# Attention and squared-ReLU MLP on one core: a maximum traced ahead of a subtraction, and v loaded a head sooner

## The chip, the cores and the metric

The kernel runs on one core of a Trainium2 chip. The metric is the device time of one execution in microseconds (us), and lower is better. Before the change the median of three executions is 1206.76 us (1206.62 to 1213.95). The engines are called PE (TensorE, matmuls), PEld (its weight loads), DVE (VectorE), ACT (ScalarE), POOL (GpSimd) and SP (SyncE, which here only issues transfers).

## The reference

Sixty-four heads (8 batches of 8) of causal attention with a decay, 576 positions, 64 columns each; then an MLP over 4608 tokens.

```python
scores = scale * np.matmul(q, k.transpose(0, 1, 3, 2))
cum = np.cumsum(np.log(np.clip(f, 0.0001, 1.0)), axis=-1)
scores = np.where(causal, -1000000000.0, scores + cum[:, :, :, None] - cum[:, :, None, :])
scores = scores - np.max(scores, axis=-1, keepdims=True)
attn = np.exp(scores)
attn = attn / (np.sum(attn, axis=-1, keepdims=True) + 1e-09)
attn_out = np.matmul(attn, v)
h = np.maximum(x @ w_in, 0.0)          # x is attn_out, heads side by side, (4608, 512)
out = (h * h @ w_out)                  # w_in (512, 2048), w_out (2048, 512)
```

The weights are double precision in memory; everything else is single precision.

## The kernel before, in words

The 64 heads are worked off one after the other, each in six slots (`NU` = 6). In a slot a head's scores are made for one stretch of queries and keys (`score`, L423 to L433), ACT turns them into exponentials (L440), and two slots later they are multiplied with v (`av_part`, L487, or L466 to L468 from head 16 on). One head ahead of its scores, each row's maximum is found from a cheaper matmul: `max_units` makes six units a head, each of them a matmul on PE (L376) into a PSUM bank and a reduction on DVE out of that bank (L384, two instructions, the second of which writes the result column `tcol`). The next user of the bank has to wait for the reduction. From the point at which the MLP's chunk 1 begins until chunk 2 begins, scores and maxima take turns in only two banks, so that a unit's matmul waits for the reduction of the unit before it.

How q and k are prepared depends on the head. Heads 0 to 9 load them rounded through POOL's queue (`load_rounded`, L292) and whole through SP's (`load_whole`, L299), and their scores are one matmul of unrounded numbers. For heads 10 to 63, `load` (L277) brings one raw tile `qkraw`, of which there is only one buffer, and `prep` splits it in four parts: part 0 rounds q and k on DVE (L321, L322) and copies the rounded k by a transfer (L323), part 1 copies the rounded q by another (L327), part 2 subtracts the rounded k from the raw one and part 3 does the same with q. For heads 10 to 19 the two subtractions run on DVE (L329 and L333, 64 x 576 each). From head 20 on `prep_split` does them on POOL.

v is loaded per head into a tile `v` of three buffers (`load_v`: the transfer L306 on SP, and on POOL a memset of its last two columns, L308). The tile comes free when the matmuls with v of the head three before are done.

Beside attention runs the MLP, chunk by chunk (L591, L606 to L609, L621), and, until about 220 us, the conversion of its weights on ACT and DVE (L206 to L242), whose loads (L195, 512 KB each) go through SP.

The order of PE, ACT, DVE and POOL is the order in which the program is traced (`in_order`). It is laid out by slots: `at(n, half, ...)` puts a step into the first or second half of slot n, and steps that fall into one half are traced in the order in which `at` was called. So the order of the calls in the loop over heads matters, not only the numbers in them. SP's order is left to the scheduler of the tile framework. An SP row that has to wait holds up everything behind it. Before the change the calls for a split head put part 1 and part 2 of `prep` into slot 1, second half, where the first maximum (unit 0) also falls, and part 3 into slot 3, second half, with unit 4; slots here count from the start of the head before.

Of the kernel before, what the change touches and what calls it, by code (L numbers as in the profile page):

```python
# [34 lines left out]
def decay_attention_relu2_kernel(  # L35
# [38 lines left out]
    NWHOLE = 10  # L74
# [195 lines left out]
    NU = len(UNITS)  # L270
# [407 lines left out]
    SPLIT = 0, 1, 1, 3  # L678
    LOAD = 4
    VLOAD, VSPLIT = 2, 4  # L680
# [56 lines left out]
    def at(n, half, do, *args):  # L737
        events.setdefault((n, half), []).append(lambda: do(*args))
# [6 lines left out]
    for h in range(NH):  # L745
        split = h >= NWHOLE
        if split:
            at((h - 2) * NU + LOAD, 0, load, h)
            for part in range(4):
                at((h - 1) * NU + SPLIT[part], 1, prep, h, part)  # L750
        else:
            if h > 1:
                at((h - 3) * NU + 3, 0, load_rounded, h)
                at((h - 2) * NU + 5, 1, load_whole, h)
        at((h - 1) * NU + VLOAD, 1, load_v, h)
        at((h - 1) * NU + VSPLIT, 1, split_v, h)
        for i, x in enumerate(MAXIMA[split]):
            at((h - 1) * NU + int(x), int(2 * x) % 2, max_unit, h, i)
        if not split:
            at((h - 1) * NU + (4 if h else 3), 0, turn_maxima, h)  # L760
    for b in range(B):
# [25 lines left out]
    for n in range(-2 * NU, last_slot + 1):  # L787
        live = 0 <= n < len(slots)
        split_last()
        if live:  # L790
            h, u = slots[n]
# [65 lines left out]
```

## Time and profile before

| | us |
|---|---|
| median of three executions | 1206.76 |
| the profiled execution | 1208.21 |
| its span, first to last instruction | 1206.5 |
| PE busy | 1178.1 (98%) |
| DVE busy | 784.9 (65%) |
| ACT busy | 684.6 (57%) |
| POOL busy | 316.9 (26%) |
| mean granted TensorE clock | 0.997 |

Busy shares are of the whole span; in the stretch from 90 to 260 us, where the weights are converted beside attention and MLP, DVE is busy for about 83% of the time, and nearly without a gap for stretches of ten or more. A timeline row gives the start in us, the duration in us, the engine, the line and the tiles, written tile first; in brackets stands how long the engine was idle before it and what ended that. A row of a wait table gives who waited for whom, us in total, how often, and the longest. In a table of stretches each engine has its busy time and its count, and at the end stand the granted clock, the DMA share and the GB/s.

### The profile page before, as it was taken

How to read it: one execution, taken by the hardware profiler on the slowest of the kernel's cores; microseconds unless marked ns; L12 is line 12 of the kernel's file. 1: busy time of each engine (PE TensorE's matmuls, PEld its weight loads, DVE VectorE, ACT ScalarE, POOL GpSimd, SP SyncE). 2: the span in 40 equal slices, each digit the busy share in tenths (PEclk: the TensorE clock that was granted, in tenths of full speed). 3: DMA queues.
4: the chain of work that ended last, by engine and by line, in shares of the span. 5: the costliest groups of instructions: out<-in, count | busy, mean ns of one | idle time of the engine just before them, and what ended most of it. 6: DMA issues, size and time to landing. Idle time of an engine off the chain costs nothing. (4 is left out here: it accounts for less than half of the span.)

```text
span 1206.5 us, 23195 instructions
## 1 busy us (share of the span) xinstructions
PE 1178.1 (98%) x7786; PEld 1040.9 (86%) x7786; DVE 784.9 (65%) x2096; ACT 684.6 (57%) x1716; POOL 316.9 (26%) x511
## 2 busy tenths in 40 slices
PE   8999999999999999999999999999999999999998
PEld 4667877789998989899999899988999899999997
DVE  5889987766766676666656667666666766543332
ACT  3765555546666566656565566666566666533232
POOL 2110000213434343422222343334333434200000
PEclk9999999999999999999999999999999999999999
DMA  7785722221212121111110212112121112000000
GB/s 204 194 209 165 196 54 46 74 67 35 51 42 60 42 55 43 50 42 35 36 50 17 59 38 54 38 43 59 42 54 36 47 42 59 12 28 18 1 19 18
DMA packets 109798, 73.33 MB, mean 61 GB/s; under 512 B 90720, under 2 KB 90720, under 8 KB 109680
## 3 DMA queue, kind: packets, MB, share of 16 engines
q1 hardware_dynamic: 108880, 68.90, 22.4%
q0 software_dynamic: 800, 2.95, 1.1%
q8 instruction: 62, 1.02, 0.4%
q14 instruction: 56, 0.46, 0.1%
HBM read 58.71 MB, written 9.87 MB: 57 GB/s over the span
## 5 line engine op out<-in xcount | busy, mean ns | idle before, releaser
L621 PE MATMUL bank<-w,gh 128*128 128x512 f32 x1152 | 413.5, 399 | 0.0
L591 PE MATMUL bank<-xh,w 128*128 128x256 f32 x2304 | 331.6, 286 | 5.3 <-ACT r L606 5.1
L591 PEld LDWEIGHTS bank<-xh,w 128*128 128x128 f32 x2304 | 300.1, 189 | 16.8 <-ACT r L606 9.3
L456 DVE TENSOR_TENSOR pl<-p,ph 128x320 fp32r<-128x320 f32 (+4 forms) x288 | 175.4, 610 | 200.6 <-ACT ph L455 195.1
L621 PEld LDWEIGHTS bank<-w,gh 128*128 128x128 f32 x1152 | 217.5, 189 | 37.9
L621 PE MATMUL bank<-w,gl 128*128 128x512 f32 x576 | 227.1, 394 | 0.2 <-DVE gl L609 0.2
L455 ACT CAST ph<-p 128x320 fp32r<-128x320 f32 (+4 forms) x288 | 119.4, 415 | 162.0 <-POOL p L442 119.2
L607 DVE TENSOR_TENSOR g<-r 128x256 f32<-128x256 f32 x288 | 124.3, 432 | 102.0 <-ACT r L606 101.7
L442 POOL TENSOR_SCALAR_AFFINE_SELECT p<-p 128x128 f32<-128x128 f32 (+1 forms) x240 | 85.9, 358 | 396.1 <-ACT p L440 328.2
L606 ACT ACTIVATE r<-bank 128x256 f32<-128x256 f32 x288 | 109.7, 381 | 137.1 <-PE bank L591 124.5
L591 PE MATMUL bank<-xl,w 128*128 128x256 f32 x1152 | 184.8, 283 | 0.0
L440 ACT ACTIVATE p<-bank 128x320 f32<-128x320 f32 (+4 forms) x288 | 111.2, 386 | 117.9 <-PE bank L428 105.9
L384 DVE CUSTOM_DVE_ANT_0 bank<-bank,mz 128x256 f32<-128x256 f32 (+4 forms) x320 | 133.6, 431 | 50.6 <-PE bank L376 50.2
L609 DVE TENSOR_TENSOR gl<-g,gh 128x256 fp32r<-128x256 f32 x288 | 139.1, 483 | 34.4 <-PE bank L621 1.0
L591 PEld LDWEIGHTS bank<-xl,w 128*128 128x128 f32 x1152 | 158.5, 191 | 0.2 <-DVE xl L577 0.2
L608 ACT ACTIVATE gh<-r 128x256 fp32r<-128x256 f32 x288 | 120.4, 418 | 9.2
L376 PE MATMUL bank<-rk 66*128 66x320 f32 (+4 forms) x384 | 109.1, 314 | 13.4 <-DVE tcol L384 8.4
L621 PEld LDWEIGHTS bank<-w,gl 128*128 128x128 f32 x576 | 109.2, 190 | 15.0 <-DVE gl L609 1.7
L428 PE MATMUL bank<-rl 128*128 128x320 f32 x324 | 95.1, 294 | 0.0
L425 PE MATMUL bank<-rk 67*128 67x320 f32 x324 | 93.4, 288 | 0.0
L376 PEld LDWEIGHTS bank<-rk 66*128 66x128 f32 (+1 forms) x384 | 67.1, 181 | 30.4 <-DVE tcol L384 12.8
L466 PE MATMUL bank<-pl,vh 128*65 128x320 f32 (+4 forms) x336 | 91.3, 272 | 0.0
(97 smaller groups left out, 1478.8 us busy)
## 6 DMA issues: line engine op xcount, KB each, us to landing
qkraw<-in_qk SPq DMA_DIRECT2D x54, 288.0 KB
v<-in_v SPq DMA_DIRECT2D x64, 160.0 KB
out<-osb SPq DMA_DIRECT2D x36, 256.0 KB
den<-rdr SPq DMA_DIRECT2D x62, 144.0 KB
w<-in_w_in SPq DMA_DIRECT2D x16, 512.0 KB
w<-in_w_out SPq DMA_DIRECT2D x16, 512.0 KB
rk<-tcol SPq DMA_DIRECT2D x216, 0.5 KB
rl<-in_qk SPq DMA_DIRECT2D x10, 288.0 KB
```

Source lines behind the costliest of these rows:

```text
L376: nc.tensor.matmul(ps[:m, :n], st["r2"][:D + 2, q0:q0 + m], st["kl0"][:D + 2, k0:k0 + n], start=True, stop=True,)
L384: nc.vector.tensor_tensor_reduce(out=ps[:m, :n], in0=ps[:m, :n], in1=mz[:m, mo:mo + n], op0=ALU.add, op1=ALU.min, scale=-1.0, scalar=init, ...
L428: nc.tensor.matmul(ps[:kn, :n], st["l2"][:, k0:k0 + kn], st["r1"][:, q0:q1], start=False, stop=not added,)
L440: nc.scalar.activation(out=p[:kn, :n], in_=ps[:kn, :n], func=AF.Exp, scale=SCALE)
L455: nc.scalar.copy(out=ph[:kn, :n], in_=p[:kn, :n])
L456: nc.vector.tensor_tensor(out=pl[:kn, :n], in0=p[:kn, :n], in1=ph[:kn, :n].bitcast(F32), op=ALU.subtract,)
L591: nc.tensor.matmul(ph[:, :T], w[:, s, cc], x[:, cc, :], start=(cc == 0 and k == 0), stop=(cc == NCC - 1 and k == 2),)
L606: nc.scalar.activation(out=r, in_=ph[:, :T], func=AF.Relu)
L607: nc.vector.tensor_tensor(out=g, in0=r, in1=r, op=ALU.mult)
L608: nc.scalar.activation(out=gh, in_=r, func=AF.Square)
L609: nc.vector.tensor_tensor(out=gl, in0=g, in1=gh.bitcast(F32), op=ALU.subtract)
L621: nc.tensor.matmul(po, g[:, ts], w[:, s], start=(fc == 0 and k == 0), stop=(fc == NF - 1 and k == 2),)
```

## The change: two steps called elsewhere in the loop over heads

For split heads (10 and up) the four calls of `prep` move behind those of `max_unit`. Nothing else about them changes, so they stay in their slots and halves. For heads 10 to 19 this exchanges, on DVE, the first reduction with the subtraction of k, and the fifth with the subtraction of q; part 1's transfer of r1 also comes behind unit 0 in the trace. For heads 20 to 63 the neighbours are on different engines, and each engine's own order stays. The second edit puts `load_v` of heads 2 to 9 six slots (one head) earlier.

```diff
         split = h >= NWHOLE
         if split:
             at((h - 2) * NU + LOAD, 0, load, h)
-            for part in range(4):
-                at((h - 1) * NU + SPLIT[part], 1, prep, h, part)
         else:
...
-        at((h - 1) * NU + VLOAD, 1, load_v, h)
+        at((h - (2 if 1 < h < NWHOLE else 1)) * NU + VLOAD, 1, load_v, h)
         at((h - 1) * NU + VSPLIT, 1, split_v, h)
         for i, x in enumerate(MAXIMA[split]):
             at((h - 1) * NU + int(x), int(2 * x) % 2, max_unit, h, i)
+        if split:
+            for part in range(4):
+                at((h - 1) * NU + SPLIT[part], 1, prep, h, part)
```

On DVE, in the preparation of head 18 (rl, qkraw and rk are its q and k; bank and tcol belong to the maxima; g and gl to the MLP), before:

```order
L607 TENSOR_TENSOR g<-r 128x256
L609 TENSOR_TENSOR gl<-g,gh 128x256
L329 TENSOR_TENSOR rl<-qkraw,rk_79 64x576
L384 ISA bank_3031,tcol<-bank_3031,mz 128x256
L384 ISA tcol 128x1
L384 ISA bank_3044,tcol<-bank_3044,mz,tcol 128x320
```

and after, at the same place:

```order
L607 TENSOR_TENSOR g<-r 128x256
L609 TENSOR_TENSOR gl<-g,gh 128x256
L384 ISA bank_3029,tcol<-bank_3029,mz 128x256
L384 ISA tcol 128x1
L329 TENSOR_TENSOR rl<-qkraw,rk_79 64x576
L384 ISA bank_3044,tcol<-bank_3044,mz,tcol 128x320
```

Unit 0's reduction and its result stand ahead of the subtraction now, and unit 1's reduction behind both as it did. The same happens at the other nine heads, and with L333 and unit 4; these twenty exchanges are all that changes on DVE. PE's and ACT's orders do not change.

On SP, at the start of the program (v_263 is v of head 1, v_358 that of head 2; w are weights, rl and rk q and k), before:

```order
L195 DMA w4_247<-in_w_in 128x1024
L306 DMA v_263<-in_v 128x5x64
L286 DMA rk_1_80<-cum_dr_85 2x576
L195 DMA w5_307<-in_w_out 128x1024
L299 DMA rl_81<-in_qk 64x1152
L286 DMA rl_81<-cum_dr_85 2x576
L306 DMA v_358<-in_v 128x5x64
```

and after (v_269 is v of head 2, v_364 that of head 3):

```order
L195 DMA w4_247<-in_w_in 128x1024
L306 DMA v_263<-in_v 128x5x64
L306 DMA v_269<-in_v 128x5x64
L286 DMA rk_1_80<-cum_dr_85 2x576
L195 DMA w5_310<-in_w_out 128x1024
L299 DMA rl_81<-in_qk 64x1152
L286 DMA rl_81<-cum_dr_85 2x576
L306 DMA v_364<-in_v 128x5x64
```

One transfer of v is added behind that of head 1, and at each later place where v of a head was loaded, that of the next head is loaded, up to head 9; the place at which v of head 9 was loaded is gone. POOL's memsets of v move in the same way. The other rows of SP keep their order up to there. Behind it the scheduler has exchanged some neighbours. For one, the load of head 13's raw q and k stands, before, behind the last row of head 12's maxima (the one of 64):

```order
L389 DMA rk_79<-tcol 1x128x1 x2
L195 DMA w_2267<-in_w_in 128x1024
L389 DMA rk_79<-tcol 1x128x1
L389 DMA rk_79<-tcol 1x64x1
L277 DMA qkraw<-in_qk 64x1152
```

and after, ahead of it:

```order
L389 DMA rk_79<-tcol 1x128x1 x2
L277 DMA qkraw<-in_qk 64x1152
L389 DMA rk_79<-tcol 1x64x1
L286 DMA rk_80<-cum_dr 2x576
L195 DMA w_2366<-in_w_out 128x1024
```

The load of qkraw, which waits for the subtraction of q that reads the same buffer, no longer waits for the last maximum as well.

## Prediction

> **What bounds the kernel now.** The page's head and its first row say that PE is the engine to look at: of the span it is idle for 28.4 us in all.
>
> ```profile
> span 1206.5 us, 23195 instructions
> PE 1178.1 (98%) x7786; PEld 1040.9 (86%) x7786; DVE 784.9 (65%) x2096; ACT 684.6 (57%) x1716; POOL 316.9 (26%) x511
> ```
>
> An edit that removes no PE work can therefore only win idle time of PE. The second view is the table of PE's own waits (us in total, times, longest):
>
> ```profile
> PE bank L376 <- DVE tcol L384: 8.4, 8, 1.7
> PE bank L591 <- ACT r L606: 5.1, 8, 0.8
> PE bank L376 <- DMA rk<-cum_dr: 2.6, 1, 2.6
> PE bank L487 <- DMA v<-in_v: 2.0, 1, 2.0
> PE bank L487 <- ACT w L211: 1.2, 1, 1.2
> ```
>
> The first row is a maximum's matmul that waits for the reduction of the unit before it; the fourth is a first matmul with v. These are the two waits that the two edits touch. The third view is PE's timeline, for where the eight waits of the first row stand.
>
> ```profile
> 135.13 0.41 PE L376 MATMUL bank<-rk 66*128 66x320 f32 x1 [0.23 <-DVE tcol L384]
> 158.31 0.24 PE L376 MATMUL bank<-rk 66*64 66x64 f32 x1 [0.97 <-DVE tcol L384]
> 169.99 0.42 PE L376 MATMUL bank<-rk 66*128 66x320 f32 x1 [1.05 <-DVE tcol L384]
> 190.84 0.41 PE L376 MATMUL bank<-rk 66*128 66x320 f32 x1 [0.68 <-DVE tcol L384]
> 194.20 0.24 PE L376 MATMUL bank<-rk 66*64 66x64 f32 x1 [0.65 <-DVE tcol L384]
> 206.38 0.41 PE L376 MATMUL bank<-rk 66*128 66x320 f32 x1 [1.41 <-DVE tcol L384]
> 223.50 0.42 PE L376 MATMUL bank<-rk 66*128 66x320 f32 x1 [1.75 <-DVE tcol L384]
> 242.65 0.42 PE L376 MATMUL bank<-rk 66*128 66x320 f32 x1 [1.62 <-DVE tcol L384]
> ```
>
> All lie between 135 and 243 us, in the preparation of heads 12 to 18. The matmuls of 64 columns are unit 5, which waits for unit 4; those of 320 are unit 1 (which waits for unit 0), but for the one at 190.84, which is unit 3. So seven of eight wait for just the reduction that the change moves ahead.
>
> **Part one, the exchange on DVE.** The fourth view is DVE's timeline at one of them, head 17:
>
> ```profile
> 221.87 0.43 DVE L609 TENSOR_TENSOR gl<-g,gh 128x256 fp32r<-128x256 f32 x1
> 222.21 0.84 DVE L329 TENSOR_TENSOR rl<-qkraw,rk 64x576 fp32r<-64x576 f32 x1
> 222.97 0.42 DVE L384 CUSTOM_DVE_ANT_0 bank<-bank,mz 128x256 f32<-128x256 f32 x1
> 223.32 0.13 DVE L384 DVE_READ_ACCUMULATOR2_ANT tcol<- 128x1 f32 x1
> 223.96 0.56 DVE L384 CUSTOM_DVE_ANT_0 bank<-bank,mz,tcol 128x320 f32<-128x320 f32 x1 [0.51 <-PE bank L376]
> ```
>
> The reduction starts 0.76 us after the subtraction started, with no gap. PE's wait of 1.75 us began at 221.75, so unit 0's matmul was long done: the reduction stood only behind the subtraction. Exchanged, it starts 0.76 earlier, and PE with it. The subtraction then falls into the gap of 0.51 that DVE has here ahead of unit 1's reduction. Unit 1 cannot come later than before: the same work stands ahead of it, and its matmul is earlier. The subtraction's result is wanted by the scores one head on, slots later, and costs nothing there. The others of these subtractions are alike:
>
> ```profile
> L329 DVE TENSOR_TENSOR rl<-qkraw,rk 64x576 fp32r<-64x576 f32 x10 | 7.6, 764 | 0.0
> L333 DVE TENSOR_TENSOR rl<-qkraw,rk 64x576 fp32r<-64x576 f32 x10 | 7.5, 752 | 0.3
> ```
>
> The mean is 764 and 752 ns, and the next instruction starts some 0.08 before the end (222.21 + 0.84 - 222.97), so each exchange brings a reduction forward by 0.67 to 0.68, and by 0.76 at head 17. A wait shrinks by that or to nothing: 0.23 (head 12), 0.68 (158.31), 0.68 (169.99), 0 (190.84, no subtraction directly ahead), 0.65 (194.20), 0.67 (206.38), 0.76 (223.50), 0.67 (242.65). The sum is 4.34 us.
>
> Not all of it need stay, since DVE is nearly full there. PE that comes earlier than DVE waits longer at the next place, unless DVE itself was waiting for what PE feeds it. At heads 16 to 18 it was (the 0.51 above is such a wait). Between 158.31 and 169.99 DVE has only two waits of note for work that comes from PE, both ahead of L607 (0.21, and 167.84 - 167.03 - 0.68, about 0.12):
>
> ```profile
> 162.49 0.43 DVE L607 TENSOR_TENSOR g<-r 128x256 f32<-128x256 f32 x1 [0.21 <-ACT r L606]
> 167.03 0.68 DVE L217 TENSOR_TENSOR w<-osb,w 128x512 fp32r<-128x512 f32 x1
> 167.84 0.42 DVE L607 TENSOR_TENSOR g<-r 128x256 f32<-128x256 f32 x1
> ```
>
> They allow DVE to come forward by 0.33, so that of PE's lead of 0.68 some 0.35 is given back. That leaves 4.0 us. Bounds: 0, if DVE gives back all, and 8.4, if the waits vanish altogether. I take 4.0, since six of the seven rows need nothing but the exchange. The load of qkraw that SP now issues ahead of the last maximum of head 12 I cost at nothing: DVE gets its raw tile sooner there, but waits for PE's unit 1 again soon after.
>
> A second gain may hang on these waits. The table of stretches (the last three columns are granted clock, DMA share, GB/s) shows a lower clock right where the wait of 1.62 at 242.65 is:
>
> ```profile
> 240.00:246.00 6.00, 4.38 (x21) 3.91 (x22) 3.47 (x11) 1.18 (x5) 0.29 (x1) 0.76 0.24 51
> 246.00:252.00 6.00, 6.00 (x37) 5.07 (x36) 4.80 (x13) 2.38 (x6) 1.09 (x2) 0.95 0.41 134
> ```
>
> The clock lost is 6 x 0.24 + 6 x 0.05 = 1.7 us, of which I count 1.5 as time. With a wait of 0.95 in place of 1.62 I expect full clock there. The Trainium skill, "TensorE: Matmul & The Clock Gate", section "HAM oscillation — how this bites in real kernels", has the abstract rule "no PE-idle gaps >~3.4µs". By that rule a gap of 1.62 would not touch the clock, the low stretch would have another cause and stay, and the sum would be 1.5 us smaller; the trace speaks against it, as the clock falls within the same 6 us in which PE was idle for 1.6.
>
> **Part two, v a head sooner.** Here the rows are two issues on SP and the two matmuls that used those tiles:
>
> ```profile
> 39.30 0.58 SPq L306 DMA_DIRECT2D v<-in_v  x1
> 45.91 0.72 PE L487 MATMUL bank<-ph,v 128*65 128x320 f32 x2 [1.18 <-ACT w L211]
> 62.84 0.59 SPq L306 DMA_DIRECT2D v<-in_v  x1
> 70.50 0.72 PE L487 MATMUL bank<-ph,v 128*65 128x320 f32 x2 [2.01 <-DMA v<-in_v]
> ```
>
> Head 6 waits 2.01 us for a transfer that took until 7.66 after its issue. Head 3 waits 1.18, and the row names a weight of ACT, which this matmul does not read; with its v issued 6.61 before, I put that down to v too. Issued at the place of the head before (for head 3 that is 27.67, a row shown below), both tiles have landed in time, and 3.2 us are free.
>
> Most of this is taken back at head 7, in my reading. Its scores need q and k by L299:
>
> ```profile
> 64.01 0.36 SPq L195 DMA_DIRECT2D w<-in_w_in  x1
> 64.79 0.48 SPq L299 DMA_DIRECT2D rl<-in_qk  x1
> 74.41 0.78 PE L423 MATMUL bank<-rl 67*128 67x320 f32 x2 [0.22 <-ACT rl L411]
> 63.00:70.00 7.00, 5.28 (x32) 3.57 (x30) 6.68 (x19) 5.61 (x14) 1.46 (x2) 1.00 0.98 235
> w<-in_w_in SPq DMA_DIRECT2D x16, 512.0 KB
> rl<-in_qk SPq DMA_DIRECT2D x10, 288.0 KB
> ```
>
> The queue is full (0.98, 235 GB/s). The v that landed by 70.4 is followed by 512 KB of weights (2.2 us at that rate) and 288 KB of q and k (1.25), so rl lands near 73.9, an estimate, against scores that start at 74.41. The change puts another head's v at that place in the queue, with the same bytes. So the queue moves forward only with its own triggers, which follow PE after head 3, by up to 1.18. The 2.01 of head 6 turns into a wait for rl. I keep 1.0 of 3.2; the bounds are 0 and 3.2.
>
> What is queued behind the moved transfers: v of head 3 takes a place at 27.67 on SP, and its buffer is that of head 0, whose last matmul is the second row here.
>
> ```profile
> 27.67 0.55 SPq L306 DMA_DIRECT2D v<-in_v  x1
> 29.27 0.38 PE L487 MATMUL bank<-ph,v 128*65 128x128 f32 x2
> 31.09 0.25 SPq L286 DMA_DIRECT2D rk<-cum_dr  x1
> ```
>
> SP now waits there until 29.65, and the row behind it (L286) did not start until 31.09 for a reason of its own. So the wait is free, and later heads have more room. POOL's memset waits likewise, ahead of a load (L292) that waits longer for PE. The extra 160 KB at the start come out at 0.7 us of the queue (at 235 GB/s), behind the transfers that PE waits for at 19.73, and I cost them at nothing.
>
> **The sum.** The profiled execution took 1208.2 us around its span of 1206.5: 1208.2 - 4.0 - 1.0 - 1.5 = 1201.7. It stands 1.45 over the median of 1206.76, about the low-clock stretch, which the median execution may not have had: 1206.76 - 5.0 = 1201.8. I forecast 1201.8.
>
> **The rivals.**
> - *All of v's gain stays* (rl is not what holds head 7, only ACT's copy L411, which the row names). Then 4.0 + 3.2 = 7.2, and 1199.6. For it: the row's own words. Against: 0.22 of wait shows that something was late there already while PE was late too. Chance 0.15.
> - *The gain is given back* (DVE, converting weights, sets the pace from 135 to 220, and the wait moves from unit 1 to unit 3, as at 190.84, where PE waited 0.68 with no subtraction directly ahead). Then perhaps 1.0 of part one and none of part two stay: 1205.8. For it: the two small gaps ahead of 169.99. Against: DVE's gap of 0.51 at head 17. Chance 0.19.
> - *Slower: SP is held up by the early v.* If a tile comes free later than the next row of SP could start, everything behind it is late, and q and k of heads 3 to 9 with it. Its price is up to 31.09 - 29.65 = 1.4 of room lost and then more; with 2.0 us (27.67 to 29.65) at each of seven heads, of which head 7 alone showed no room and the others about 1, some 2 + 6 x 1 = 8 us are added, less the 4.0 of part one: 1210.8. It decides as soon as the release lies behind the next row's own start; the rows for head 3 say it does not. Chance 0.08.
>
> **How the numbers follow.** The forecast has 0.58, with 1200 to 1204 as its own range. Its neighbours reach 1199.6, less 1.5 if the median had the low-clock stretch (1198.1), and 1205.8; the median before moved by 0.1 to 7 us between executions, so I stretch both ends a little: 1197.8 to 1207.5 leaves out the slower rival and some scatter, 0.18 in all. About 1% (12 us) is what a measurement can tell from no change. Faster than 1194.7 needs both upper bounds: 0.04. Slower than 1218.8 needs more than the third rival: 0.03. Within 1%: 0.93.
>
> **What would show it.** In the profile after, PE's row for L376 behind L384 falls from 8.4 to 4 or 5 us, with the unit 5 waits near 0 and 0.3, and those of heads 16 to 18 each 0.7 smaller. The rows for L487 behind v and behind L211 are gone. A new wait of 1 to 2 us stands ahead of head 7's first score (L423), now near 73.4. The clock is full at 240 to 250. Wrong would be: no wait at head 7 (first rival), waits of L376 that merely moved to unit 2 or 3 (second), or SP rows L286 and L299 later against PE than before (third).

## The result, and the profile after

The changed kernel takes 1202.62 us (median of 20 executions, 1197.7 to 1210.1); the kernel before took 1208.17 us beside it (median of 20, 1206.1 to 1218.05). The ratio is 0.9947, with a 95% interval of 0.9928 to 0.9966: the change saves between 0.3% and 0.7%. The head of the profile after, and the rows of PE's own waits that answer to those of before (us in total, times, longest):

```profile
span 1204.9 us, 23192 instructions
PE 1180.4 (98%) x7786; PEld 1042.1 (86%) x7786; DVE 785.1 (65%) x2096; ACT 684.7 (57%) x1716; POOL 317.4 (26%) x511
...
PE bank L591 <- ACT r L606: 5.5, 9, 0.8
PE bank L376 <- DVE tcol L384: 4.5, 6, 1.0
PE bank L376 <- DMA rk<-cum_dr: 1.7, 1, 1.7
...
PE bank L423 <- DMA rl<-in_qk: 1.5, 1, 1.5
PE bank L423 <- DMA rl<-cum_dr: 1.4, 1, 1.4
```

The wait of the maxima fell from 8.4 to 4.5 us. The rows of L487, the first matmul with v, are gone (3.2 us). Two waits of L423, a head's first score, are new: 2.9 us. At the start PE waited 2.59 us for head 1's decay rows; now it waits 1.06 for head 0's and 1.70 for head 1's. PE's timeline of the changed kernel has them in their places:

```profile
57.93 0.78 PE L423 MATMUL bank<-rl 67*128 67x320 f32 x2 [1.36 <-DMA rl<-cum_dr]
74.39 1.38 PE L423 MATMUL bank<-rl 67*128 67x320 f32 x2 [1.53 <-DMA rl<-in_qk]
142.40 0.50 PE L376 MATMUL bank<-rk 66*128 66x320 f32 x2 [0.21 <-DVE tcol L384]
148.76 0.39 PE L425 MATMUL bank<-rk 67*128 67x320 f32 x1 [0.24 <-DMA rk<-tcol]
172.72 0.41 PE L376 MATMUL bank<-rk 66*128 66x320 f32 x1 [0.99 <-DVE tcol L384]
193.42 0.42 PE L376 MATMUL bank<-rk 66*128 66x320 f32 x1 [0.67 <-DVE tcol L384]
207.66 0.41 PE L376 MATMUL bank<-rk 66*128 66x320 f32 x1 [0.73 <-DVE tcol L384]
224.20 0.42 PE L376 MATMUL bank<-rk 66*128 66x320 f32 x1 [0.99 <-DVE tcol L384]
242.64 0.42 PE L376 MATMUL bank<-rk 66*128 66x320 f32 x1 [0.95 <-DVE tcol L384]
```

There is no matmul of 64 columns left among the rows of L376: of the two waits of unit 5 (0.97 and 0.65) one is gone and 0.13 is left of the other. The wait of 0.23 at head 12's unit 1 is gone too, but its unit 3 now waits 0.21 (142.40), and its first score (L425) waits 0.24 for a row of its maxima, which it did not before. The waits of unit 1 in heads 16 to 18 are 0.73, 0.99 and 0.95, where they were 1.41, 1.75 and 1.62, so each is smaller by 0.67 to 0.76, the length of a subtraction. DVE's timeline at head 17 has the exchange itself:

```profile
223.32 0.43 DVE L609 TENSOR_TENSOR gl<-g,gh 128x256 fp32r<-128x256 f32 x1
223.66 0.43 DVE L384 CUSTOM_DVE_ANT_0 bank<-bank,mz 128x256 f32<-128x256 f32 x1
224.00 0.14 DVE L384 DVE_READ_ACCUMULATOR2_ANT tcol<- 128x1 f32 x1
224.00 0.75 DVE L329 TENSOR_TENSOR rl<-qkraw,rk 64x576 fp32r<-64x576 f32 x1
224.67 0.55 DVE L384 CUSTOM_DVE_ANT_0 bank<-bank,mz,tcol 128x320 f32<-128x320 f32 x1
```

Unit 0's reduction follows L609 at once, PE's matmul starts at 224.20, and the subtraction runs beside it. Unit 1's reduction follows without the gap of 0.51 that stood there before.

The span alone hides this gain: 1204.9 is only 1.6 us less than the 1206.5 of before. The rest is clock. The table of stretches, cut into pieces of 3.41 us, shows it (the last three columns are granted clock, DMA share and GB/s; the first number after the length is PE's busy time). Of before:

```profile
17.88:21.29 3.41, 1.56 (x9) 1.32 (x10) 0.99 (x5) 0.42 (x2) 0.00 (x0) 1.00 1.07 350
21.29:24.70 3.41, 3.41 (x13) 2.22 (x12) 3.30 (x14) 1.61 (x5) 0.91 (x2) 0.50 0.69 217
...
239.75:243.16 3.41, 1.63 (x10) 1.26 (x11) 2.80 (x9) 0.94 (x3) 0.29 (x1) 1.00 0.40 90
243.16:246.57 3.41, 3.41 (x16) 3.17 (x15) 1.49 (x6) 0.80 (x2) 0.00 (x0) 0.50 0.02 0
```

And of after:

```profile
16.40:19.81 3.41, 1.71 (x8) 1.04 (x7) 0.40 (x2) 0.44 (x1) 0.00 (x0) 1.00 1.12 214
19.81:23.22 3.41, 3.41 (x15) 2.54 (x13) 2.59 (x10) 1.32 (x3) 0.00 (x0) 0.50 1.04 381
23.22:26.63 3.41, 3.41 (x11) 1.73 (x9) 2.98 (x9) 1.21 (x3) 0.51 (x1) 0.50 1.04 303
...
53.93:57.34 3.41, 2.64 (x17) 1.65 (x15) 2.43 (x8) 2.69 (x8) 0.57 (x1) 1.00 0.90 179
57.34:60.75 3.41, 2.82 (x14) 2.01 (x15) 2.02 (x7) 2.06 (x6) 0.00 (x0) 1.00 0.70 181
71.01:74.42 3.41, 1.88 (x16) 1.30 (x14) 1.77 (x3) 2.36 (x7) 0.00 (x0) 1.00 1.14 214
74.42:77.83 3.41, 3.41 (x8) 2.18 (x9) 1.67 (x7) 1.38 (x4) 0.00 (x0) 0.50 0.61 117
77.83:81.24 3.41, 3.41 (x13) 2.40 (x11) 2.04 (x6) 1.63 (x4) 0.10 (x1) 0.50 0.63 172
...
241.67:245.08 3.41, 2.46 (x18) 2.34 (x18) 2.53 (x8) 0.89 (x3) 0.22 (x1) 1.00 0.32 68
```

The clock is either full or half, and it changes at the edges of such pieces. Before, two pieces ran at half clock; after, four. With PE busy throughout, half a clock for 6.8 us costs 3.4 us, for 13.7 us it costs 6.8. Without them the two profiled executions would have spans of about 1206.5 - 3.4 = 1203.1 and 1204.9 - 6.8 = 1198.1, which is 5.0 apart.

### The profile page after: what moved, and what is told of

The parts are those of the page before. It is cut to its first block, busy times and chain, and to the rows that moved or that the text cites. A ratio compares the mean times of both kernels' runs of the same rounds, so it can differ in the third digit from the quotient of the medians.

```text
span 1204.9 us, 23192 instructions
## 1 busy us (share of the span) xinstructions
PE 1180.4 (98%) x7786; PEld 1042.1 (86%) x7786; DVE 785.1 (65%) x2096; ACT 684.7 (57%) x1716; POOL 317.4 (26%) x511
## 5 line engine op out<-in xcount | busy, mean ns | idle before, releaser
L607 DVE TENSOR_TENSOR g<-r 128x256 f32<-128x256 f32 x288 | 125.7, 436 | 100.2 <-ACT r L606 100.2
L606 ACT ACTIVATE r<-bank 128x256 f32<-128x256 f32 x288 | 109.7, 381 | 133.8 <-PE bank L591 118.0
L609 DVE TENSOR_TENSOR gl<-g,gh 128x256 fp32r<-128x256 f32 x288 | 133.2, 463 | 33.3
L608 ACT ACTIVATE gh<-r 128x256 fp32r<-128x256 f32 x288 | 120.5, 418 | 9.1
L376 PE MATMUL bank<-rk 66*128 66x320 f32 (+4 forms) x384 | 110.6, 318 | 9.6 <-DVE tcol L384 4.5
L425 PE MATMUL bank<-rk 67*128 67x320 f32 x324 | 93.5, 289 | 0.2 <-DMA rk<-tcol 0.2
L467 PE MATMUL bank<-ph,v 128*64 128x320 f32 (+4 forms) x336 | 91.2, 271 | 0.0
```

The costliest lines, as they stand in the source:

```text
L376: nc.tensor.matmul(ps[:m, :n], st["r2"][:D + 2, q0:q0 + m], st["kl0"][:D + 2, k0:k0 + n], start=True, stop=True,)
L606: nc.scalar.activation(out=r, in_=ph[:, :T], func=AF.Relu)
L607: nc.vector.tensor_tensor(out=g, in0=r, in1=r, op=ALU.mult)
L608: nc.scalar.activation(out=gh, in_=r, func=AF.Square)
L609: nc.vector.tensor_tensor(out=gl, in0=g, in1=gh.bitcast(F32), op=ALU.subtract)
```

## The experiments

Where a kernel of the study adds or removes lines, its line numbers differ by a few from those of the changed kernel; the tiles' names are the same.

**The exchange alone** (the changed kernel, with v loaded as before):

```diff
-        at((h - (2 if 1 < h < NWHOLE else 1)) * NU + VLOAD, 1, load_v, h)
+        at((h - 1) * NU + VLOAD, 1, load_v, h)
```

> Before, with the exchange alone (v loaded where it was). Theory: the exchange carries most of the gain. PE's waits of L376 behind L384 fall from 8.4 us to about 4.5, the waits of L487 behind v stay at about 3.2, and the time is about 4 us under before (ratio 0.996 to 0.997), up to 1.5 more in executions where the low-clock stretch at 243 us goes too. Rival (v carries the gain, and the exchange only moves waits): within 1 us of before, and the waits of L376 turn up at units 2 and 3.

Measured: 1205.56 us (12 executions) against 1207.93 before (23); ratio 0.9971, 0.994 to 1.0003. Two rows of PE's waits:

```profile
PE bank L376 <- DVE tcol L384: 6.0, 8, 1.1
...
PE bank L487 <- DMA v<-in_v: 1.2, 2, 0.9
```

The interval of the ratio just reaches 1, so the times alone do not show a gain here; the section on the prediction comes back to it with the clock taken out. The waits for v are 1.2 in this execution, not the 3.2 that were expected: how long PE waits for v differs between executions even where v is loaded as before. The wait of the maxima is 6.0, not 4.5. The difference is one new wait of 1.11 at head 12 and a few tenths elsewhere (0.28 at a unit 5). PE's row of it, and the rows of DVE and POOL ahead of it, in the timeline:

```profile
127.72 1.50 POOL L523 TENSOR_TENSOR xt<-xt,den 128x576 f32<-128x576 f32 x1 [22.91 <-DVE rk L322]
...
127.86 1.65 DVE L607 TENSOR_TENSOR g<-r 128x256 f32<-128x256 f32 x1
...
130.82 0.41 PE L376 MATMUL bank<-rk 66*128 66x320 f32 x1 [1.11 <-DVE tcol L384]
```

POOL divides a finished head's output (L523), for which it reads two tiles, while DVE's L607, which multiplies r by itself, wants two operands of its own; L607 takes 1.65 us and ends 0.28 us after POOL's instruction, where it takes 0.42 otherwise. DVE is late by 1.2, and PE waits 1.1 for it. POOL's row names DVE's L322 as what ended its wait, but L523 does not read what L322 writes; what it needs are the two transfers into den (L520), and the last of these has its completions until 127.59 in the trace. So where L523 falls differs between kernels and executions. In the changed kernel's profile it falls at 134.78: L607 gets through in 0.41, the next step (L609) is held instead (1.46), and DVE is still done before unit 0's matmul, so that PE does not wait.

**v a head sooner alone** (the kernel before, with only the second edit):

```diff
-        at((h - 1) * NU + VLOAD, 1, load_v, h)
+        at((h - (2 if 1 < h < NWHOLE else 1)) * NU + VLOAD, 1, load_v, h)
```

> Before, with v of heads 2 to 9 sooner alone. Theory: v's waits (3.2 us) go, but q and k of heads 5 and 7 are waited for instead, 2.5 to 3 us, so that about 1 us is won (ratio 0.999), less whatever clock the wait at head 7 costs (the changed kernel's profile has 6.8 us at half clock right behind it). The eight waits of L376 (8.4 us) stay. Rival: the whole 3.2 us is won.

Measured: 1207.63 us (12 executions) against 1207.93; ratio 0.9992, 0.9976 to 1.0009. PE's waits:

```profile
PE bank L376 <- DVE tcol L384: 8.1, 7, 1.8
...
PE bank L423 <- DMA rl<-cum_dr: 1.1, 1, 1.1
```

The waits for v are gone here too, and the maxima wait as they did before. One wait for rl stands in their place, ahead of head 5; the one expected at head 7 is not there. So v sooner is worth little alone: nothing that this measurement can tell from zero.

**q and k of heads 2 to 9, and their decay rows, through POOL's queue**, to find out whether rl is late because it stands behind weights in SP's queue (on the changed kernel):

```diff
-        nc.sync.dma_start(out=x.raw[:D], in_=qk[h])
-        if cum:
+        engine = nc.gpsimd if h > 1 else nc.sync
+        engine.dma_start(out=x.raw[:D], in_=qk[h])
+        if cum and h > 1:
+            engine.dma_start(out=f32(x.k[D + 1:D + 3, :S]), in_=cum_dr[h])
+        elif cum:
```

> The changed kernel, with q and k of heads 2 to 9 (L299) and their decay rows issued on POOL's queue and not on SP's. Theory: they come late at heads 5 and 7 because they stand behind weights in SP's queue. Then PE's waits of L423 behind them (1.4 and 1.5 us) fall under 0.5 in all, the half-clock stretch behind head 7 goes, and the time is 2.5 us under the changed kernel's at full clock, and up to 3.4 more against executions that have that stretch (ratio to before about 0.991). Rival: the 16 transfer engines are full there, whichever queue a load stands in; then the waits stay at 2.5 to 3 us and the time is the changed kernel's.

Measured: 1220.87 us (4 executions), ratio 1.0106, 1.0093 to 1.0119. Neither expectation held. The worst of PE's timeline, at head 7's first score, and the issue rows of POOL for it, with the row ahead of them:

```profile
75.98 1.40 POOL L526 TENSOR_TENSOR xt<-xt,den 128x576 f32<-128x576 f32 x1 [4.59 <-DMA den<-rdr]
77.34 0.57 POOL L300 DMA_DIRECT2D rl<-in_qk  x1
77.91 0.51 POOL L302 DMA_DIRECT2D rl<-cum_dr  x1
...
87.16 1.41 PE L426 MATMUL bank<-rl 67*128 67x320 f32 x2 [5.75 <-DMA rl<-cum_dr]
```

The scores waited 5.75 us here, and 8.3 us in all at two heads; the clock, with 0.985 in the mean, paid for it a second time. Two things made these loads late. They stand on POOL right behind the division of a finished head (L526), which had itself waited 4.59 us for a transfer; and the two small decay rows then landed at 87.02, 9.1 us after their issue (the median of all eight such transfers is 6.3 us for 4.5 KB). So the experiment put the load behind POOL's own work and into a queue whose transfers take their own time, and it says nothing on the place in SP's queue.

**Nine idle matmuls in PE's wait at 19 us.** The 13.7 us of half clock in the profile of v alone and the first 6.8 us in that of the changed kernel both begin right behind PE's wait for head 1's decay rows. `spin(n)` is the kernel's own filler: n matmuls of zeros whose result nobody reads.

```diff
+    events.setdefault((0, 0), []).insert(0, lambda: spin(9))
     spin(36)
```

> The changed kernel, with nine dummy matmuls (L768, about 1.8 us) in PE's wait at 17 to 19 us. Theory: the half clock that both profiles show from about 20 us on (3.4 us long before, 6.8 after) follows that wait. Then the clock stays full there, the work under it takes 1.7 to 3.4 us less, and the time is 1.7 to 3.4 us under the changed kernel's. Rival: a wait of 1.7 to 2.6 us does not touch the clock, which falls for another reason; then the low stretch stays and the time is the changed kernel's, or up to 0.5 us over it.

Measured: 1200.8 us (6 executions, 1198.09 to 1206.13), ratio 0.9949, 0.9928 to 0.9969. In the profile PE has no wait at this place any more and the clock is full up to the last microseconds (mean 0.999, span 1197.1). The ratio is that of the changed kernel (0.9947), so this run alone does not show the gain that was expected. The same kernel once more, on another chip:

> The kernel with nine dummy matmuls in the early wait once more, for its clock over more executions, and as the base of the two runs beside it. Theory: it beats the changed kernel only by clock: at full clock both take about 1199, and its mean granted clock is near 0.998 against 0.996, so its median lies about 2 us lower. Rival: the clock varies as before, and the medians are equal within 1 us.

Measured: 1199.27 us (6 executions, 1197.71 to 1201.26) against 1206.43; ratio 0.9928, 0.9903 to 0.9952. This is the lowest ratio of the study, but its interval still overlaps that of the changed kernel (0.9928 to 0.9966), so a gain over the changed kernel is not shown by the times. What is shown is the clock at this place: it is full behind the filled wait in all four traces with the nine matmuls, and half behind the unfilled wait in four of the five others (the fifth, of the exchange alone, waited 1.27 us there, the shortest). The mean clock is 0.998 over the twelve executions with the nine matmuls and 0.996 over the twenty of the changed kernel. The second run's profile has one low stretch:

```profile
77.00:84.00 7.00, 7.00 (x23) 4.64 (x22) 5.09 (x11) 4.26 (x12) 1.25 (x1) 0.54 0.96 277
```

No wait of PE stands ahead of it, so waits do not explain every low stretch. Ten matmuls of a single column (L541) run just before. They are not enough by themselves: the same ten run in every trace of the study, in seven others also wholly within one piece of 3.41 us, and no half clock follows there. The cause stays open.

**Weights behind q and k in SP's queue** (on the kernel with the nine matmuls): each 512 KB weight load of heads 2 to 7 is held back until the next load of rl is issued.

```diff
-                nc.sync.dma_start(out=raw, in_=(w_in, w_out)[i % 2][i // 2].bitcast(I32))
+                held.append(lambda: nc.sync.dma_start(out=raw, in_=(w_in, w_out)[i % 2][i // 2].bitcast(I32)))
+                release()
...
+        if n % NU == NU - 1:
+            release(True)
```

> The kernel with dummy matmuls, and the weights' loads of heads 2 to 7 traced right behind the load of q and k (L299) in place of wherever their conversion asks for them. Theory: what gives back v's gain is that head 7's q and k stand behind weights in SP's queue. Then they land 1 to 2 us sooner, head 7's first score no longer starts just 1.2 us after the last packet of its load, and at full clock the time is 0.5 to 1.5 us less than with the dummy matmuls alone. Rival: the queue is full whatever its order, and the load lands no sooner; then the time is the same within 0.5 us, or a weight comes late and it is more.

Measured: 1201.59 us (12 executions), ratio 0.9961, 0.9936 to 0.9985. From head 6's first score to head 7's, 7.1 us pass rather than the 7.9 of the kernel without this edit: rl does come sooner if no weights stand ahead of it. But from head 4's to head 5's it is 8.1 rather than 7.1 to 7.5, from head 7's to head 8's 9.7 rather than 8.4, and a wait of 0.7 at a maximum ahead of head 5 is new. The time is no better: what head 7 gains, other heads lose.

**The subtractions of heads 10 to 19 on POOL** (on the kernel with the nine matmuls), to take them out of DVE's way altogether (`prep_split` also makes the two copies on ACT in place of the transfers L323 and L327):

```diff
-        if h >= NPLAIN + 4:
-            prep_split(h, part)
-            return
+        prep_split(h, part)
+        return
```

> The kernel with dummy matmuls, and heads 10 to 19 prepared as the later heads are: the two subtractions on POOL, the two copies on ACT, no transfers for them. Theory: the exchange has taken from the waits of L376 what the subtractions cost, and what is left (4.5 us) is other DVE work. Then the waits stay between 3.5 and 4.5 us, and the time at full clock is within 1 us. Rival (DVE's total load sets the pace there, and the exchange only shifted it): with 15 us less on DVE the waits fall under 2 us and the time by 2 to 4 us.

Measured: 1210.09 us (12 executions), ratio 1.0024, 1.0002 to 1.0046: 10.8 us over the kernel that it was made from (1199.27 beside it); with the clock taken out as described in the next section it is 7.2 (5.8 to 8.5). The expectation, waits of 3.5 to 4.5 us and the same time within 1 us, did not hold. PE's waits, and the timeline at head 18:

```profile
PE bank L375 <- DVE tcol L383: 9.6, 6, 2.2
...
238.25 1.99 POOL L350 TENSOR_TENSOR rl<-qkraw,rk 64x576 fp32r<-64x576 f32 x1 [0.76 <-DVE rk L343]
...
238.89 1.63 DVE L606 TENSOR_TENSOR g<-r 128x256 f32<-128x256 f32 x1
...
240.97 0.43 DVE L383 CUSTOM_DVE_ANT_0 bank<-bank,mz 128x256 f32<-128x256 f32 x1
...
241.51 0.63 PE L375 MATMUL bank<-rk 66*128 66x320 f32 x1 [2.18 <-DVE tcol L383]
```

The subtraction is not gone from DVE's way: it takes 1.99 us on POOL instead of 0.75 on DVE, and DVE's L606 takes 1.63 rather than 0.42 and ends 0.28 us behind it. So the reduction starts later than if DVE had done the subtraction first. It is the same ahead of each of the six waits: a DVE step there is stretched to between 0.83 and 1.81 us. The waits of the maxima are 9.6 us rather than 4.4, and one MLP matmul waits 1.5 for a stretched L608: together 6.7 of the 7.2. What the copies on ACT add was not tried apart.

## Why the prediction was right, point by point

Predicted were 1201.8 us and a gain of 5.0 over the median; measured are 1202.62 and 1208.17 - 1202.62 = 5.55. The result is within 1%, as was given a chance of 0.93. That the two numbers are so close is partly luck, as the clock shows.

*Apart from the clock.* The executions differ mostly by clock: over all 131 whose clock is known, time grows by 1.19 us for each 0.001 of mean granted clock that is lost (a straight line with one constant per run; the kernel before has one for each of two chips), and 0.001 of 1200 us is 1.2. At full clock that line gives 1203.4 and 1202.3 for before on the two chips, 1198.6 for after, 1200.6 for the exchange alone, 1202.6 for v alone and 1198.8 and 1198.2 with the nine matmuls, each within 0.7 to 1.1 (95%). On which chip the changed kernel ran is not on record. The change is worth 4.9 or 3.7 by the one chip or the other, each within 0.8, and 4.3 by both together; the prediction's 4.0 and 1.0 were 5.0. The rest of the measured 5.55 is clock and scatter. The nine matmuls add nothing at full clock.

*The exchange, 4.0.* The mechanism held: eight waits of 8.36 us became six of 4.54, which is 3.8 less, and 0.24 came back at head 12's first score. At heads 15 to 18 each wait came out as in the sum (0.65, 0.68, 0.76 and 0.67 less, and nothing at unit 3 of head 15). Elsewhere the sum was right and its terms were not. At head 12 0.23 was to be won, but the wait moved to unit 3. At head 13 the wait of 0.97 vanished almost wholly, where 0.29 was to stay. What was won there beyond the forecast was lost at 169.99: the wait became 0.99 in place of 1.05, so that of a lead of 0.68 not 0.35 but 0.62 was given back. Alone, against before on the same chip, the exchange is worth 2.9 within 0.9 in the line above. Its one profile has 1.1 of wait behind DVE's instruction beside L523, which may be why it falls short of 4.0; more than one execution would be needed to show it.

*v a head sooner, 1.0 of 3.2.* The size is right. The early clock had left the changed kernel 0.93 us behind (the same matmul at 26.65, before at 25.72); at head 7's first score it is 0.02 ahead (74.39 against 74.41), so 0.95 was won in between. The wait for rl came as described: at 74.39, 1.53 long, foreseen as 1 to 2 us near 73.4. But the forecast kept all of head 3's gain and gave back all of head 6's, and that split was wrong. The lead was 1.33 after head 3's wait went, and head 5's wait for its rl took back 1.30; it rose by 2.2 where head 6's wait went, and head 7 took back 1.65. So the step that failed is "the queue moves forward only with its own triggers, which follow PE after head 3": SP issued head 5's q and k at 51.14 rather than 49.72, 1.4 us later, although PE stood 0.4 earlier at 45.51. That what was kept adds up to 1.0 all the same is luck. On the first rival: head 7's first score starts 1.2 to 1.3 us behind the last packet of its rl in before, after, and three of the experiments, and 1.7 to 2.6 behind it in three others, but never sooner; which speaks for rl having held head 7 in before too, and not the ACT copy that the row names. Alone, against before on the same chip, v is worth 0.9 within 0.9. The two parts apart, 2.9 and 0.9, and both together with the nine matmuls on that chip, 4.6 within 1.2, do not differ by more than the uncertainty.

*The half-clock stretch at 243, 1.5.* It went, as the row of 241.67 shows: with 0.95 us of idleness the clock stayed full. The other traces bear it out: half clock follows where the wait at head 18 is 1.6 or more (before, v alone, the subtractions on POOL), and full clock where it is 0.95, but for one trace, in which the wait of 0.48 just ahead fell into the same piece (1.43 us together). That was the step in which the Trainium skill's "TensorE: Matmul & The Clock Gate", section "HAM oscillation — how this bites in real kernels", spoke against the forecast with its gaps of over 3.4 us; the rows of 16.40, 71.01 and 239.75 have 1.53 to 1.78 us of idleness and half clock behind each. The step was applied in one place only, and this is the prediction's real omission: a new wait of 1 to 2 us at head 7 was forecast, and by the very same rule it had to cost clock too. It did (6.8 us at half clock from 74.42). And the early wait of 1.70 was followed by 6.8 us of half clock, where before one of 2.59 was followed by 3.4. So in these two profiles the clock moved against the change, by 3.4. Over the executions it did not: the mean clock is 0.996 for the changed kernel and 0.995 to 0.996 for the kernel before.

*The parts costed at nothing.* The early v cost SP no room. These are its rows after:

```profile
30.66 0.55 SPq L306 DMA_DIRECT2D v<-in_v  x1
32.03 0.25 SPq L286 DMA_DIRECT2D rk<-cum_dr  x1
```

L306 waited for the matmul that frees its buffer, and L286 behind it started 0.94 us later than the 31.09 of before, which is just the 0.93 by which everything was later there. So the third rival, a slower kernel by SP held up, fell. The load of qkraw ahead of the last maximum, also costed at nothing, may not be free: head 12's first score waits 0.24 for a row of its maxima, 1.00 in the first profile with the nine matmuls and 0.84 with the weights behind, and not at all in before and in three other traces with the new order on SP. These rows were issued just ahead of that load; whether the load makes them land later is not shown. The second rival, with the gain given back by DVE, is false for the kernel as changed, but for the 0.2 that moved to unit 3 of head 12.

## What to carry to other kernels

Where two engines take turns in two buffers, put the step that the other engine waits for ahead of any step that nobody wants yet; the gain is the length of the exchanged step at each wait, up to the wait itself, less what the next wait takes back where the reading engine has no gap. A transfer that is made earlier frees its own wait, but in a full queue look for the next one. And in this kernel a PE wait cost twice where it left PE idle for 1.5 us or more in one piece of the clock's time: splitting or filling such a wait can save its second cost, the clock, but not the wait itself.

## What the runs showed of the hardware

**The clock.** In all nine traces the half clock came in lengths of 3.4 us or a multiple (3.4 to 13.7), on a grid of 3.41 us that lies elsewhere in each execution; the first microseconds of a program, for which the traces have no clock, and the last, where PE's work runs out, are left aside here. Each of the eleven pieces of the grid in which PE was idle for 1.53 us or more was followed by half clock; between 1.3 and 1.5 both were seen (half after 1.32, 1.39 and 1.43, full after 1.31, 1.38, 1.42, 1.45 and 1.49); below 1.3 none was, but for the stretch at 77 us shown above. It is the sum within a piece that counts, not the wait: the wait of 1.36 ahead of 57.93 falls into the two pieces of 53.93 and 57.34 with 0.77 and 0.59 us of idleness, and the clock stayed full. The two waits of 0.48 and 0.95 at head 18 were followed by half clock in the one trace where they fell into one piece. This would explain why one kernel's executions lie from 1197.7 to 1210.1, with clocks from 1.000 down to 0.990: the same waits fall now into one piece, now into two. The executions that were not profiled do not show where their waits fell. Why a low stretch lasts one piece or two or four, with PE busy throughout, was not settled.

**DVE beside POOL.** A DVE step of the MLP with two operands of 128 x 256 (L607, L609) takes 0.42 us alone. Where POOL had begun an instruction that reads two tiles and DVE's step had to wait, it took up to 1.69 us (175 times in the nine traces), and each time it ended 0.28 to 0.29 us behind POOL's (240.52 against 240.24 in the last experiment). Reductions that read from a PSUM bank kept their time (0.43 for 128 x 256). It goes the other way too: where L607 came first, POOL's division took 1.87 us rather than 1.41 (134.78 in the changed kernel's profile). The Trainium skill, "SBUF — State Buffer", section "SBUF: two separate sides", states this as an exclusive lock, held for a whole instruction, of a port pair that the two share; the traces agree. So a step of 0.75 us moved from DVE to POOL can cost DVE 1.2.
